# Linear attention and a Fourier feed-forward block on one core: the first part in a fixed written order, q loaded in 768-byte packets

## The chip, the core and the metric

One core of a Trainium2 chip runs the whole program. The metric is the device time of one execution in microseconds (us); lower is better. The core has five engines with a queue of instructions each (PE multiplies matrices, DVE, ACT and POOL work on vectors, SP only issues transfers), and 16 DMA engines move data.

## What is computed

```python
kv  = einsum('bhsd,bhse->bhde', k, v)        # q, k, v: 8 x 8 x 576 x 64, float32
out = einsum('bhsd,bhde->bhse', q, kv)
out = out / sqrt(mean(out*out, -1) + 1e-6) * g_norm
x   = out.transpose(0, 2, 1, 3).reshape(8, 576, 512)
u   = x + real(fft(fft(x, axis=1), axis=2))
un  = (u - mean(u)) / sqrt(var(u) + 1e-6)    # over the last axis
y   = u + maximum(un @ w_ch1, 0) @ w_ch2     # 512 x 2048 and 2048 x 512
```

## The kernel before

The program has two parts. The first goes through the 8 batches: for each it makes kv, turns q, multiplies the two, normalizes, does both Fourier transforms as matrix products, writes u, and turns u into the form the feed-forward block reads. Beside that it converts the first weight columns and does a first piece of the feed-forward block (three of 16 column groups) for all nine token blocks. The second part, from line L1791 on, does the rest of the feed-forward block. It is nearly all 512-column matrix products.

The first part is written as a list of operations (`op` and `dma` in class `Plan`), each with an engine, a rank and the operations it needs. `Plan.run` orders them: before, it walked a made-up time, kept a list of ready operations for each engine and took the one with the smallest rank; a table `SHIFT` moved the ranks. The order so found is fixed for each engine (`pin`), so that an engine takes its instructions strictly in that order. PE stands still where the next one in its order isn't ready, though a later one might be.

What PE does in the first part, by line:

- L798, `plan_spare`: "spare" 512-column products that nothing reads. 30 stand at the start (`WARM`), and further ones (`SPARE`, two lots of 40 and 22) have the lowest rank, so the plan puts them where nothing else is ready.
- L950, `plan_kv`: kv. An operation is one pair of heads, 12 products of 64 rows by 64 columns, which the profile records as 24. Each writes half of the columns of the array. ACT copies the result (`kvt`, L961); for batch 0 DVE also writes a copy times g_norm (L970).
- L1019, `plan_q`: q turned, four products by an identity, in plain float32. ACT copies the result into `fq` (L1023).
- L1046, `plan_out`: q times kv. 16 products (32 records), each of which reads 64 partitions, that is half of the rows of the array; the two heads of a pair lie in the two halves.
- L1280 (`plan_seq`), L1324 (`plan_chn`), L1422 (`plan_turn`), L685 (weights' mean): transforms, turning and the conversion of weights.
- L726 and L744 (`plan_early`): the 512-column products of the feed-forward block, in fp32r.

`plan_q_load` (L986, L994) loads q with `p j h d` on the tile's side: each packet is 64 floats, 256 bytes, one head of one token. In the loop over batches a `plan_q` is made for each j (token modulo 3), and `plan_out` for t needs the two q tiles of its own t.

Of the kernel before, what the change touches and what calls it, by code (L numbers as in the profile page):

```python
# [14 lines left out]
ALU = mybir.AluOpType  # L15
# [12 lines left out]
NA = 3  # L28
# [15 lines left out]
SPARE = ((40, 12000), (22, 38000))  # L44
# [10 lines left out]
SHIFT = {  # L55
    ("", "DVE", -100): -2880.5,
    ("", "POOL", -40): -937,
    ("", "SP DMA", -40): -23730.5,
    ("", "HOST", 0): -1181.5,
    ("", "POOL", 10): 24,  # L60
    ("", "SP DMA", 10): 294.5,
    ("", "POOL", 20): 552.5,
    ("", "SP DMA", 20): -63868.5,
    ("", "POOL", 30): 1213.5,
    ("", "POOL", 40): 1162.5,
    ("", "POOL", 50): 2073,
    ("", "POOL", 60): 3539,
    ("", "POOL", 70): 6370.5,
    ("", "DVE", 85): -240,
    ("", "PE", 85): 1946,  # L70
    ("", "SP DMA", 85): 991.5,
    ("", "HOST", 9000): 139.5,
    ("chn", "ACT", -34): 315,
    ("chn", "DVE", -34): 25,
    ("chn", "PE", -34): 3750.5,
    ("chn", "SP DMA", -34): 18885,
    ("chn", "ACT", 16): 1136,
    ("chn", "DVE", 16): 22530.5,
    ("chn", "PE", 16): 7,
    ("chn", "POOL", 16): -981.5,  # L80
    ("chn", "SP DMA", 16): -292,
    ("chn", "ACT", 26): 3465.5,
    ("chn", "DVE", 26): 18.5,
    ("chn", "PE", 26): -28.5,
    ("chn", "SP DMA", 26): -1643.5,
    ("chn", "DVE", 36): 36.5,
    ("chn", "PE", 36): -334.5,
    ("chn", "POOL", 36): -148,
    ("chn", "SP DMA", 36): -641.5,
    ("chn", "ACT", 46): 72966,  # L90
    ("chn", "DVE", 46): 404.5,
    ("chn", "PE", 46): -656,
    ("chn", "POOL", 46): 769,
    ("chn", "SP DMA", 46): 2653,
    ("chn", "ACT", 56): -555,
    ("chn", "DVE", 56): -1076,
    ("chn", "PE", 56): 57521.5,
    ("chn", "POOL", 56): -191.5,
    ("chn", "SP DMA", 56): -527,
    ("chn", "ACT", 66): -18.5,  # L100
    ("chn", "DVE", 66): 19,
    ("chn", "PE", 66): 259.5,
    ("chn", "POOL", 66): -733.5,
    ("chn", "SP DMA", 66): -1681.5,
    ("chn", "ACT", 76): 28.5,
    ("chn", "DVE", 76): 521,
    ("chn", "PE", 76): 1380.5,
    ("chn", "POOL", 76): -141,
    ("chn", "SP DMA", 76): 1068,
    ("dft", "POOL", -37): -79,  # L110
    ("dft", "SP DMA", -37): -552.5,
    ("dft_d", "ACT", -35): -1247.5,
    ("dft_d", "DVE", -35): 2333.5,
    ("dft_d", "POOL", -35): -601,
    ("dft_rest", "POOL", 9): 1006,
    ("dft_rest", "SP DMA", 9): 7159,
    ("dft_split", "ACT", -37): 22716,
    ("dft_split", "POOL", -37): 1615,
    ("dft_split", "ACT", 9): 73006,
    ("dft_split", "POOL", 9): -14.5,  # L120
    ("early", "ACT", -100): -25,
    ("early", "DVE", -100): 2547,
    ("early", "SP DMA", -100): 400,
    ("early", "PE", 1000): 43.5,
    ("early", "PE", 1010): 3621,
    ("early", "PE", 1030): 720,
    ("early", "PE", 1040): -417,
    ("early", "PE", 1050): 53.5,
    ("early", "PE", 1060): -22,
    ("early", "PE", 1080): 47.5,  # L130
    ("fold", "DVE", -36): -1056.5,
    ("fold", "DVE", 14): 381,
    ("fold", "DVE", 24): 647,
    ("fold", "DVE", 34): 185,
    ("fold", "DVE", 44): 345.5,
    ("fold", "DVE", 54): -1436,
    ("fold", "DVE", 64): 417.5,
    ("fold", "DVE", 74): 53.5,
    ("folds", "ACT", 14): 165.5,
    ("folds", "POOL", 14): 480.5,  # L140
    ("folds", "POOL", 24): 171,
    ("folds", "ACT", 34): -184.5,
    ("folds", "POOL", 34): -317.5,
    ("folds", "ACT", 44): 1688.5,
    ("folds", "POOL", 44): -766.5,
    ("folds", "ACT", 54): 1295,
    ("folds", "POOL", 54): -440.5,
    ("folds", "ACT", 64): -1095.5,
    ("folds", "ACT", 74): -52.5,
    ("folds", "POOL", 74): -932.5,  # L150
    ("kv", "ACT", -40): -43,
    ("kv", "ACT DMA", -40): 1273,
    ("kv", "PE", -40): 878,
    ("kv", "SP DMA", -40): -36291.5,
    ("kv", "ACT", 10): -555,
    ("kv", "PE", 10): -4098.5,
    ("kv", "SP DMA", 10): -7696,
    ("kv", "ACT", 20): -544,
    ("kv", "PE", 20): -203,
    ("kv", "SP DMA", 20): 2621.5,  # L160
    ("kv", "PE", 30): 578,
    ("kv", "SP DMA", 30): 17834,
    ("kv", "ACT", 40): 1666.5,
    ("kv", "PE", 40): 3652.5,
    ("kv", "SP DMA", 40): 29857.5,
    ("kv", "ACT", 50): -2667.5,
    ("kv", "PE", 50): -60,
    ("kv", "SP DMA", 50): 1468.5,
    ("kv", "ACT", 60): -718,
    ("kv", "PE", 60): 1184.5,  # L170
    ("kv", "SP DMA", 60): 74007,
    ("kv", "ACT", 70): 950.5,
    ("kv", "PE", 70): -1199.5,
    ("kv", "SP DMA", 70): 92268.5,
    ("out", "ACT", -58): 77092,
    ("out", "DVE", -58): 200,
    ("out", "ACT", -8): -22,
    ("out", "DVE", -8): -78,
    ("out", "ACT", 2): -7071,
    ("out", "DVE", 2): -1231,  # L180
    ("out", "ACT", 12): 1319.5,
    ("out", "DVE", 12): -606.5,
    ("out", "PE", 12): -981,
    ("out", "ACT", 22): 2327,
    ("out", "DVE", 22): 2275.5,
    ("out", "PE", 22): 277.5,
    ("out", "POOL", 22): 2917.5,
    ("out", "ACT", 32): -2157,
    ("out", "PE", 32): 418.5,
    ("out", "POOL", 32): 1264.5,  # L190
    ("out", "ACT", 42): -98,
    ("out", "DVE", 42): 374.5,
    ("out", "PE", 42): -402.5,
    ("out", "POOL", 42): 56580.5,
    ("out", "ACT", 52): -34,
    ("out", "DVE", 52): -197.5,
    ("out", "PE", 52): 4262.5,
    ("out", "POOL", 52): 2493,
    ("out", "PE", 62): 1265.5,
    ("out", "POOL", 62): -863.5,  # L200
    ("out", "PE", 72): -402.5,
    ("out", "POOL", 72): 2316.5,
    ("q", "ACT", -39): 70,
    ("q", "PE", -39): -2780,
    ("q", "POOL", -39): 1767,
    ("q", "PE", 11): 936.5,
    ("q", "POOL", 11): 250.5,
    ("q", "ACT", 21): -440,
    ("q", "PE", 21): -816,
    ("q", "POOL", 21): 2781,  # L210
    ("q", "ACT", 31): -127.5,
    ("q", "PE", 31): 3763.5,
    ("q", "POOL", 31): -635,
    ("q", "ACT", 41): 143.5,
    ("q", "PE", 41): -179,
    ("q", "POOL", 41): 154,
    ("q", "ACT", 51): 1602,
    ("q", "PE", 51): 620.5,
    ("q", "POOL", 51): 4526.5,
    ("q", "ACT", 61): 3768.5,  # L220
    ("q", "PE", 61): 1082.5,
    ("q", "POOL", 61): -550.5,
    ("q", "ACT", 71): 924,
    ("q", "PE", 71): 4825,
    ("q", "POOL", 71): 54,
    ("q_load", "SP DMA", -39): -23057.5,
    ("q_load", "SP DMA", -38): -28773.5,
    ("q_load", "SP DMA", 11): -1479.5,
    ("q_load", "SP DMA", 21): 1231,
    ("q_load", "SP DMA", 31): 8702,  # L230
    ("q_load", "SP DMA", 41): 19825,
    ("q_load", "SP DMA", 51): 22558,
    ("q_load", "SP DMA", 61): 68611,
    ("q_load", "SP DMA", 71): 72453.5,
# [124 lines left out]
class Plan:  # L359
# [81 lines left out]
    def run(self):  # L441
# [5 lines left out]
        need = {}  # L447
# [1933 lines left out]
```

## Time and profile before

| | |
|---|---|
| median of 3 runs | 961.81 us (960.96 to 961.81) |
| the profiled execution's own time | 962.68 us |
| its span, first to last instruction | 960.9 us |
| PE busy | 951.0 us, 99% of the span, 5934 matmuls |
| DVE, POOL, ACT busy | 683.9, 443.7, 383.6 us |
| chain that ended last | PE 94%, DMA 2%, DVE 2%, issue 1%, SPq 1% |

Busy time on PE holds whatever is in the array, useful or not, and a matmul's end is modelled, so 99% does not say that 99% is needed. The rate (how many matmuls in how many us) says more.

### The profile page before, as it was taken

What the parts mean: (1) busy time and instruction counts of PE and PEld (TensorE: products, weight loads), DVE (VectorE), ACT (ScalarE), POOL (GpSimd) and SP (SyncE); (2) the same over time, 40 slices, a digit from 0 to 9 for tenths busy, and PEclk for the clock granted to TensorE, in tenths of its full rate; (3) what the DMA queues carried; (4) which work ended last, traced back from release to release, by engine and by line L of the source; (5) the groups of instructions that cost most, each with busy time, mean ns of one, the idle gap of its engine ahead of it and who ended that gap; (6) DMA issues with size and microseconds to landing.
All of it is one profiled execution on the core that took longest, in us unless ns stands there. A gap on an engine that the chain in (4) does not pass through costs nothing.

```text
span 960.9 us, 15968 instructions
## 1 busy us (share of the span) xinstructions
PE 951.0 (99%) x5934; PEld 799.0 (83%) x5934; DVE 683.9 (71%) x1199; ACT 383.6 (40%) x719; POOL 443.7 (46%) x436
## 2 busy tenths in 40 slices
PE   9999999999999999999999999999999999999998
PEld 7888889888888888888888888888888888888886
DVE  4889776678797478999457967586757685675554
ACT  2666766758655233433314321351225212521110
POOL 3557778676764215556725044825472437210000
PEclk9999999999999999999999999999999999999999
DMA  9999995955447899988489397529643675213412
GB/s 241 224 225 270 234 296 156 307 125 197 152 151 247 323 335 339 339 302 299 169 341 330 116 376 252 206 66 310 238 154 105 232 279 194 89 66 135 184 63 88
DMA packets 112654, 210.39 MB, mean 219 GB/s; under 512 B 45292, under 2 KB 66688, under 8 KB 103616
## 3 DMA queue, kind: packets, MB, share of 16 engines
q1 hardware_dynamic: 109536, 199.92, 63.1%
q0 software_dynamic: 1920, 6.29, 1.8%
q10 hardware_dynamic: 1120, 3.15, 1.1%
q8 instruction: 47, 0.77, 0.3%
q14 instruction: 31, 0.25, 0.1%
HBM read 141.40 MB, written 67.93 MB: 218 GB/s over the span
## 4 chain that ended last, share of the span: by engine, by line
PE 94%; DMA 2%; DVE 2%; issue 1%; SPq 1%; POOL 0%; ACT 0%; DVEq 0%; POOLq 0%
PE acc L2188 23%; PE ps_h L2153 20%; PE ps_h L1791 11%; PE acc L1802 10%; PE acc L744 8%; PE ps_h L726 7%; PE ps_f L1280 3%; PE ps_o L1046 3%; PE ps_f L1324 2%; PE ps_k L950 2%; PE ps_s L798 2%; DMA vm<-in_v_dram 2%; PE ps_t L1422 1%; PE ps_q L1019 1%; DMA km<-in_k_dram 1%
## 5 line engine op out<-in xcount | busy, mean ns | idle before, releaser
L2188 PE MATMUL acc<-w2c,hh 128*128 128x512 f32 x640 | 197.7, 390 | 0.0
L739 DVE SCALAR_TENSOR_TENSOR hl<-ps_h,hh 128x512 fp32r<-128x512 f32 x144 | 98.5, 687 | 103.6 <-ACT hh L736 103.2
L736 ACT ACTIVATE hh<-ps_h 128x512 fp32r<-128x512 f32 x144 | 85.8, 597 | 216.4 <-PE ps_h L2153 89.9
L2188 PEld LDWEIGHTS acc<-w2c,hh 128*128 128x128 f32 x640 | 119.7, 188 | 25.4
L2198 DVE TENSOR_TENSOR us<-acc,us 128x512 f32<-128x512 f32 (+1 forms) x161 | 106.9, 681 | 42.3 <-PE acc L2188 41.9
L2188 PE MATMUL acc<-w2c,hl 128*128 128x512 f32 x320 | 124.5, 389 | 0.0
L2153 PE MATMUL ps_h<-t,w1c 128*128 128x512 f32 x480 | 115.3, 389 | 0.0
L2153 PEld LDWEIGHTS ps_h<-t,w1c 128*128 128x128 f32 x480 | 90.1, 188 | 18.7
L1824 POOL TENSOR_TENSOR us<-us,low 128x512 f32<-128x512 f32 x30 | 45.6, 1524 | 99.3 <-ACT low L1821 93.4
L2153 PE MATMUL ps_h<-b,w1c 128*128 128x512 f32 x360 | 91.2, 389 | 0.0
L2153 PEld LDWEIGHTS ps_h<-b,w1c 128*128 128x128 f32 x360 | 67.6, 188 | 14.0
L2188 PEld LDWEIGHTS acc<-w2c,hl 128*128 128x128 f32 x320 | 60.1, 188 | 12.4
L726 PE MATMUL ps_h<-unTh,w 128*128 128x512 f32 x216 | 67.6, 395 | 1.3 <-DVE hl L739 1.3
L744 PE MATMUL acc<-w,hh 128*128 128x512 f32 x216 | 67.8, 399 | 0.0
L1802 PE MATMUL acc<-w,hh 128*128 128x512 f32 x216 | 64.2, 390 | 0.0
L1791 PE MATMUL ps_h<-unTh,w 128*128 128x512 f32 x192 | 59.9, 393 | 0.0
L2019 POOL TENSOR_TENSOR z<-z,low 128x512 f32<-128x512 f32 x24 | 31.0, 1296 | 58.4 <-DMA low<-unT_scr 58.3
L1096 POOL TENSOR_TENSOR x<-x,gb 96x512 f32<-96x512 f32 (+1 forms) x36 | 46.1, 1302 | 10.6 <-ACT x L1063 10.4
L2170 DVE TENSOR_TENSOR ps_h<-ps_h,s 128x512 f32<-128x512 f32 x60 | 39.8, 693 | 13.8 <-PE ps_h L2153 13.2
L2255 ACT COPY s<-ps_h 128x512 f32<-128x512 f32 x20 | 11.7, 587 | 92.5 <-PE ps_h L2153 92.5
L726 PEld LDWEIGHTS ps_h<-unTh,w 128*128 128x128 f32 x216 | 39.7, 188 | 9.5 <-DVE hl L739 1.5
L1802 PEld LDWEIGHTS acc<-w,hh 128*128 128x128 f32 x216 | 40.5, 188 | 8.3
(207 smaller groups left out, 1969.1 us busy)
## 6 DMA issues: line engine op xcount, KB each, us to landing
w1c<-w_scr SPq DMA_DIRECT2D x13, 1792.0 KB
raw<-in_moe_w_ch_dram SPq DMA_DIRECT2D x32, 512.0 KB
w2c<-w_scr SPq DMA_DIRECT2D x14, 1024.0 KB
unT_scr<-unTh SPq DMA_DIRECT2D x9, 1024.0 KB
unT_scr<-unTl SPq DMA_DIRECT2D x9, 1024.0 KB
part_scr<-part SPq DMA_DIRECT2D x36, 256.0 KB
w_scr<-w1q SPq DMA_DIRECT2D x5, 1792.0 KB
km<-in_k_dram SPq DMA_DIRECT2D x29, 288.0 KB
```

The lines of the kernel that those rows point to most:

```text
L726: nc.tensor.matmul(ps, w[c][:, kc * P : (kc + 1) * P], unT[a][:, kc, :], start=(idx == 0), stop=(idx == 3 * KC - 1),)
L736: nc.scalar.activation(hh, ps, AF.Relu)
L739: nc.vector.scalar_tensor_tensor(hl, ps, 0.0, hh.bitcast(F32), ALU.max, ALU.subtract)
L744: nc.tensor.matmul(acc, hpair[a][:, i * P : (i + 1) * P], w[c], start=(first and n == 0), stop=(last and n == 2),)
L1096: nc.gpsimd.tensor_tensor(v_, v_, gb[:n].unsqueeze(1).to_broadcast([n, H, D]), ALU.mult)
L1791: nc.tensor.matmul(ps, w1_of(f, c, kc), unTs[j][a][:, kc, :], start=(idx == 0), stop=(idx == 3 * KC - 1),)
L1802: nc.tensor.matmul(acc, hpair[a][:, i * P : (i + 1) * P], w2_of(f, c), start=(first_ and n == 0), stop=(last_ and n == 2),)
L1824: nc.gpsimd.tensor_tensor(ut, ut, part, ALU.add)
L2153: nc.tensor.matmul(ps, w[:, A_OF[m], c, kc * P : (kc + 1) * P], b[:, a, kc * BT : (kc + 1) * BT], start=(fresh and idx == 0), stop=(done a ...
L2170: nc.vector.tensor_tensor(to, a, b, ALU.add)
L2188: nc.tensor.matmul(ps, hpair[a][:, i * P : (i + 1) * P], w2c[n][:, r, c], start=(idx == 0), stop=(idx == 5),)
L2198: nc.vector.tensor_tensor(ut[:, cols], ps[:, cols], ut[:, cols], ALU.add)
```

## The change

- `run` takes the operations in the order of a string `ORDER`, two digits an operation. `SHIFT` and the ready lists are gone. The made-up time stays, for the rings of buffers and for `pin`.
- `SPARE` has 33 and 10 in place of 40 and 22: 19 spares fewer. `WARM` stays.
- q lies in its tile as `p h j d`, so that a packet is three tokens of one head: 192 floats, 768 bytes. Batch 0 has two loads a side (by heads) in place of three (by token), the other batches one as before; the broadcast row loads three tokens.
- `plan_q` turns 128 of the 192 columns (j, d) of each pair, so that a tile `fq` holds two of six pieces (head, token); `plan_out` takes its piece from the half where it lies. For that kv must lie in both halves: `kvt` has two slots, and three copies a batch take the place of one (on ACT; for batch 0 also on DVE). There are still six q tiles a batch and 16 products an output.
- Rings: fq 6 for 4, kv 5 for 6, e2 4 for 5. `plan_chn` also waits for the row sums of x (`zs`).

```diff
-SPARE = ((40, 12000), (22, 38000))
+SPARE = ((33, 12000), (10, 38000))
...
+ORDER = (
+    "040G0Z1H4l1N0U0K0F0O0P0E0A05071b0I1M0R1G0M0W0D020X1j1i0T09060Q0B0C4m4x0V1K084n0S0L1O4o1P4p1I1J4q0N0J"
...
-        for o in self.ops:
-            if not o.after:
-                heapq.heappush(events, (0, o.n, "ready", o))
...
+        digits = [DIGITS.index(c) for c in ORDER]
+        order = [self.ops[64 * a + b] for a, b in zip(digits[::2], digits[1::2])]
...
+        for o in order:
+            t = max([0] + [a.done + (0 if a.eng == o.eng else self.HOP) for a in o.after]) + o.wait
+            t = max(t, free.get(o.eng, 0), port if o.port else 0)
...
+            self.pin(o.emit, t)
...
-        kvt = ring("kvt", qkv, [P, NPAIR, D], "kvt")
+        kvt = ring("kvt", qkv, [P, 2, NPAIR, D], "kvt")
...
+        parts = ((0, 0, 0, P), (1, 0, D, D), (1, D, 0, D))
...
+        done = [op("ACT", 370, rank(b, KV), keep(*part), mm, [ps, kvt]) for part in parts]
...
-        qt = ring("qt", qkv, [TR + 2, 3, DM], "qt")
+        qt = ring("qt", qkv, [TR + 2, H, 3, D], "qt")
...
+        src = q[b, :, t0 : t0 + HALF, :].rearrange("h (p j) d -> p h (j d)", j=3)
+        parts = 2 if b == 0 else 1
...
-                nc.tensor.transpose(view()[:, m, :], qt.t[:n, j, m * P : (m + 1) * P], ident[:n, :n])
+            flat = qt.t[:n].rearrange("p (c s) j d -> p c (s j d)", s=2)
...
+                        piece = 3 * s + (2 - t if side else t)
+                        on = slice(piece % 2 * D, (piece % 2 + 1) * D)
...
-                            fqs[side].t[half, m, :n],
-                            kvt.t[half, m],
+                            fqs[side][piece // 2].t[on, m, :n],
+                            kvt.t[on, (s + piece) % 2, m],
```

Three places show how the order moves. First PE's start. Before (`ps_s` a spare, `ps_k` kv, `ps_w` the weights' mean, `ps_q` q turned):

```order
L798 MATMUL ps_s<-still 128x512 x30
L950 MATMUL ps_k<-vm,km 64x64 x12
L685 MATMUL ps_w<-wa,mean_t 128x128 x4
L798 MATMUL ps_s<-still 128x512 x2
L950 MATMUL ps_k<-vm,km 64x64 x12
L798 MATMUL ps_s<-still 128x512
L950 MATMUL ps_k<-vm,km 64x64 x12
L798 MATMUL ps_s<-still 128x512
L950 MATMUL ps_k<-kvm 64x64 x12
L798 MATMUL ps_s<-still 128x512 x2
L1019 MATMUL ps_q<-ident,qt 128x96 x4
```

PE's start in the changed kernel:

```order
L485 MATMUL ps_s<-still 128x512 x26
L637 MATMUL ps_k<-vm,km 64x64 x24
L485 MATMUL ps_s<-still 128x512 x4
L372 MATMUL ps_w<-wa,mean_t 128x128 x4
L485 MATMUL ps_s<-still 128x512 x4
L711 MATMUL ps_q<-ident,qt 128x96 x12
L485 MATMUL ps_s<-still 128x512 x3
L637 MATMUL ps_k<-vm,km 64x64 x12
L637 MATMUL ps_k<-kvm 64x64 x12
```

The four pairs of batch 0 stood alone between spares; now they stand two and two, and the first q turns stand between them. Second, PE around the end of batch 1's kv (its last pair is the second `kvm` row). Before:

```order
L950 MATMUL ps_k<-kvm 64x64 x12
L798 MATMUL ps_s<-still 128x512 x10
L1019 MATMUL ps_q<-ident,qt 128x98 x4
L1019 MATMUL ps_q<-ident,qt 128x96 x8
L798 MATMUL ps_s<-still 128x512 x9
L1019 MATMUL ps_q<-ident,qt 128x96 x4
L798 MATMUL ps_s<-still 128x512
L1046 MATMUL ps_o<-kvt,fq 96x64 x16
```

The same place in the changed kernel:

```order
L485 MATMUL ps_s<-still 128x512
L637 MATMUL ps_k<-kvm 64x64 x12
L637 MATMUL ps_k<-vm,km 64x64 x12
L741 MATMUL ps_o<-kvt,fq 96x64 x16
L485 MATMUL ps_s<-still 128x512
L741 MATMUL ps_o<-kvt,fq 96x64 x16
L637 MATMUL ps_k<-vm,km 64x64 x12
L741 MATMUL ps_o<-kvt,fq 98x64 x16
L637 MATMUL ps_k<-vm,km 64x64 x12
```

Between batch 1's last pair and its first output stood 20 spares and four q turns; now one pair of batch 2 does. Third, the start of SP's queue of transfers. Before (`raw` weights, `km` and `kvm` k, `qt` q):

```order
L649 DMA raw<-in_moe_w_ch_dram 128x4x256
L649 DMA raw<-in_moe_w_ch_dram 128x1024
L790 DMA rowidx<-in_order_dram 128x36
L939 DMA km<-in_k_dram 96x2x384 x3
L939 DMA kvm<-in_k_dram 96x2x384
L986 DMA qt<-in_q_dram 96x8x64 x2
```

The start of SP's queue in the changed kernel:

```order
L336 DMA raw<-in_moe_w_ch_dram 128x4x256
L691 DMA qt<-in_q_dram 2x8x192
L626 DMA km<-in_k_dram 96x2x384 x2
L476 DMA gb<-in_g_norm_dram 128x64
L685 DMA qt<-in_q_dram 96x4x192 x2
L336 DMA raw<-in_moe_w_ch_dram 128x1024
L626 DMA kvm<-in_k_dram 96x2x384
L626 DMA km<-in_k_dram 96x2x384
```

One side of q now stands ahead of the second weights and of the last two pairs of k.

## Rows read from the trace of the kernel before

**Rows 1.** Windows: stretch; busy us (instructions) by engine; granted clock, DMA share, GB/s.

```profile
0.00:7.00 7.00, 5.05 (x12) 4.00 (x13) 0.54 (x5) 2.15 (x3) 1.11 (x9) 1.00 0.71 216
12.00:80.00 68.00, 65.43 (x941) 56.21 (x938) 56.26 (x114) 40.23 (x87) 34.93 (x52) 1.00 1.08 231
80.00:140.00 60.00, 59.26 (x665) 51.91 (x663) 46.60 (x96) 40.55 (x86) 45.44 (x52) 1.00 1.01 275
140.00:344.00 204.00, 202.99 (x1582) 176.15 (x1583) 147.17 (x310) 120.54 (x252) 122.95 (x135) 1.00 0.66 214
344.00:957.00 613.00, 613.00 (x2718) 506.87 (x2716) 429.46 (x671) 180.13 (x294) 237.59 (x190) 1.00 0.58 214
```

**Rows 2.** Waits of PE over the whole span: us in total, times, longest us.

```profile
PE ps_s L798 <- DVE still L793: 2.0, 1, 2.0
PE ps_h L726 <- DVE hl L739: 1.3, 1, 1.3
PE ps_k L950 <- issue: 1.1, 1, 1.1
PE ps_k L950 <- DMA vm<-in_v_dram: 0.6, 2, 0.4
PE ps_o L1046 <- DVE unTl L1434: 0.5, 2, 0.3
PE ps_k L950 <- DVE ss L1083: 0.4, 1, 0.4
PE ps_q L1019 <- DVE ss L1083: 0.4, 1, 0.4
```

**Rows 3.** Timeline of PE, pairs and q turns among spares: start us, us.

```profile
14.97 0.51 PE L798 MATMUL ps_s<-still 128*128 128x512 f32 x1
15.40 0.92 PE L950 MATMUL ps_k<-vm,km 96*64 96x64 f32 x24
16.25 0.50 PE L798 MATMUL ps_s<-still 128*128 128x512 f32 x1
...
18.10 0.49 PE L1019 MATMUL ps_q<-ident,qt 96*128 96x96 f32 x4
18.38 0.95 PE L798 MATMUL ps_s<-still 128*128 128x512 f32 x3
19.16 0.49 PE L1019 MATMUL ps_q<-ident,qt 96*128 96x96 f32 x4
```

**Rows 4.** Timeline of PE, three pairs together and two outputs together.

```profile
24.25 2.96 PE L1046 MATMUL ps_o<-kvt,fq 64*96 64x64 f32 x64
27.15 0.88 PE L1019 MATMUL ps_q<-ident,qt 96*128 96x96 f32 x8
...
160.85 2.32 PE L950 MATMUL ps_k<-vm,km 96*64 96x64 f32 x72
163.10 0.55 PE L1422 MATMUL ps_t<-ident,x 97*128 97x97 f32 x4
```

**Rows 5.** Timeline of PE, one output between 512-column products.

```profile
81.49 0.39 PE L726 MATMUL ps_h<-unTl,w 128*128 128x512 f32 x1
81.81 1.57 PE L1046 MATMUL ps_o<-kvt,fq 64*96 64x64 f32 x32
83.32 0.73 PE L726 MATMUL ps_h<-unTh,w 128*128 128x512 f32 x2
83.89 0.40 PE L726 MATMUL ps_h<-unTl,w 128*128 128x512 f32 x1
84.12 0.62 PE L726 MATMUL ps_h<-unTh,w 128*128 128x512 f32 x2
84.58 0.39 PE L726 MATMUL ps_h<-unTl,w 128*128 128x512 f32 x1
```

**Rows 6.** The tile kvt: duration ns min/median/max, first and last start us.

```profile
L961 ACT COPY kvt<-ps_k x8: 372/372/384, 17.6 to 200.6; 128x256 f32<-128x256 f32 x8
```

**Rows 7.** The page's line on DMA packets.

```profile
DMA packets 112654, 210.39 MB, mean 219 GB/s; under 512 B 45292, under 2 KB 66688, under 8 KB 103616
```

More of the change, by code (lines that the diff above doesn't have):

```diff
@@ L342 @@
+DIGITS = "0123456789ABCDEFGHIJKLMNOPQRSTUVWXYZabcdefghijklmnopqrstuvwxyz+-"
 GAIN_AT_ONCE = (1,)
 RINGS = {
-    "p8": 8, "part": 2, "unT": 2, "h": 2 * NA, "qt": 2, "fq": 4, "kvt": 2, "kv": 6, "kr": 2, "xst": 1, "x": 9, "raw": 2, "e2": 5, "wk": 2, "xhl": 3, "pt": 1, "two": 2, "far": 1,
+    "p8": 8, "part": 2, "unT": 2, "h": 2 * NA, "qt": 2, "fq": 6, "kvt": 2, "kv": 5, "kr": 2, "xst": 1, "x": 9, "raw": 2, "e2": 4, "wk": 2, "xhl": 3, "pt": 1, "two": 2, "far": 1,
 }
@@ new lines, in run @@
+        for o in order:
+            t = max([0] + [a.done + (0 if a.eng == o.eng else self.HOP) for a in o.after]) + o.wait
+            t = max(t, free.get(o.eng, 0), port if o.port else 0)
+            for b in o.bufs:
+                if b.t is None:
+                    first = min(slots[b.ring])
+                    slots[b.ring].remove(first)
+                    t = max(t, first)
+                    b.t = b.make() or True
+            self.pin(o.emit, t)
+            end = free[o.eng] = t + o.cost
+            if o.port:
+                port = end
+            if o.dma:
+                pipe = max(pipe, end + 1300) + o.lag
+                free[o.eng] = max(end, pipe - self.AHEAD)
+                end = pipe + 700
+            for b in o.bufs:
+                b.left -= 1
+                b.close = max(getattr(b, "close", 0), end)
+                if not b.left:
+                    slots[b.ring].append(b.close)
+            o.done = end
@@ L975, in plan_kv, with src, keep @@
-        scaled = op("DVE", 330, rank(b, KV), gain, mm + [i_gb], [ps, kvg])
-        return kvt, kvg, [done, scaled], ld
+        def src(lo, hi):
+            return ps.t[lo:hi, : NPAIR * D].rearrange("p (c t) -> p c t", c=NPAIR)
+        parts = ((0, 0, 0, P), (1, 0, D, D), (1, D, 0, D))
+        def keep(slot, to, lo, n):
+            return lambda: nc.scalar.copy(kvt.t[to : to + n, slot], src(lo, lo + n))
+        done = [op("ACT", 370, rank(b, KV), keep(*part), mm, [ps, kvt]) for part in parts]
@@ L978, in plan_q_load, with gain @@
+        if b:
+            return kvt, kvt, done, ld
+        kvg = ring("kvt", qkv, [P, 2, NPAIR, D], "kvt")
+        def gain(slot, to, lo, n):
+            return lambda: nc.vector.tensor_tensor(
+                kvg.t[to : to + n, slot], src(lo, lo + n),
+                gb[lo : lo + n].unsqueeze(1).to_broadcast([n, NPAIR, D]), ALU.mult,
+            )
+        done += [op("DVE", 330, rank(b, KV), gain(*part), mm + [i_gb], [ps, kvg]) for part in parts]
+        return kvt, kvg, done, ld
     def plan_q_load(b, side):
-        qt = ring("qt", qkv, [TR + 2, 3, DM], "qt")
+        qt = ring("qt", qkv, [TR + 2, H, 3, D], "qt")
@@ new lines, in plan_q_load @@
+        parts = 2 if b == 0 else 1
+        ld = []
+        for n in range(parts):
+            hs = slice(n * H // parts, (n + 1) * H // parts)
+            ld.append(dma(
+                597 / parts, rank(b, QT) + n / 4,
+                lambda hs=hs: nc.sync.dma_start(of(qt.t[:TR, hs]), src[:, hs]),
+                bufs=[qt],
+            ))
+        if not side:
+            ld.append(dma(
+                2, rank(b, QT),
+                lambda: nc.sync.dma_start(
+                    of(qt.t[TR:]), q[b, :, :3, :].rearrange("h j d -> h (j d)").partition_broadcast(2),
@@ L1005, in plan_q_load, with plan_q @@
         return qt, ld
-    def plan_q(b, side, j, qt, ld):
-        n = rows[0] if side == 0 and j == 0 else TR
+    def plan_q(b, side, m, qt, ld):
+        n = TR if side else TR + 2
         fq = ring("fq", qkv, [P, NPAIR, TR + 2], "fq")
@@ L1017, in turn @@
         def turn():
-            for m in range(NPAIR):
-                nc.tensor.transpose(view()[:, m, :], qt.t[:n, j, m * P : (m + 1) * P], ident[:n, :n])
+            flat = qt.t[:n].rearrange("p (c s) j d -> p c (s j d)", s=2)
+            for c in range(NPAIR):
+                nc.tensor.transpose(
+                    view()[:, c, :], flat[:, c, m * P : (m + 1) * P], ident[:n, :n]
+                )
         def take():
@@ L1026, in plan_q @@
         done.append(op("ACT", 490, rank(b, QT), take, [tr], [ps, fq]))
-        if side and j == 2:
+        if side and m:
             done.append(op(
@@ L1370, in plan_chn @@
         if b == 0:
-            adds = [op("DVE", 690, r, fn, pms, [x, pm], port=True) for fn in (add_l, add_r)]
+            adds = [op("DVE", 690, r, fn, pms + read, [x, pm], port=True) for fn in (add_l, add_r)]
         else:
-            adds = [op("POOL", 1240, r, fn, pms, [x, pm]) for fn in (add_l, add_r)]
+            adds = [op("POOL", 1240, r, fn, pms + read, [x, pm]) for fn in (add_l, add_r)]
         r0 = b * S + 1
@@ L1565 @@
         )
-        reds, gs, fqs = [], {}, {}
+        reds, gs, fqs, taken = [], {}, [], []
         for side in range(2):
             qt, loaded = plan_q_load(b, side)
-            for j in range(3):
-                fqs[side, 2 - j if side else j] = plan_q(b, side, j, qt, loaded[j])
+            made = [plan_q(b, side, m, qt, loaded) for m in range(3)]
+            fqs.append([f for f, _ in made])
+            taken.append([d for _, d in made])
         for t in range(3):
-            pair = [fqs[side, t] for side in range(2)]
-            d, gs[t] = plan_out(
-                b, t, [p[0] for p in pair], pair[0][1] + pair[1][1] + kvt_done + [one_row], kvt,
-                kvg, xs[t], ss,
-            )
+            need = sum((
+                taken[side][m] for side in range(2)
+                for m in sorted({(3 * s + (2 - t if side else t)) // 2 for s in range(2)})
+            ), [])
+            d, gs[t] = plan_out(b, t, fqs, need + kvt_done + [one_row], kvt, kvg, xs[t], ss)
             reds.append(d)
```

455 lines of the change are left out of this document (45 added, 410 removed).

## The prediction, made before the changed kernel ran

> **What bounds the kernel now.** I read the windows first, because PE is 99% busy on the page and busy time alone doesn't say what the array does. From 344 to 957 us PE is busy in all of 613 us with 2718 matmuls, nearly all of 512 columns [rows 1]: 613 / 2718 = 0.2255 us each, which is the rate of one such product. Nothing in the change touches this part, and it can only start earlier. So the question is the first 344 us. There PE is busy too (65.43 of 68 us at the least dense place after the start), but with three things that give no result: spares, stops at a change of the kind of product, and waits.
>
> The view of waits comes next. After the first one (2.0 us at the start, before any data, which stays) PE waits for 1.3 + 1.1 + 0.6 + 0.5 + 0.4 + 0.4 = 4.3 us in all [rows 2]. Two of these end at transfers or at "issue" on kv (0.6 and 1.1), the others at DVE. The DMA engines are full to 140 us (shares of 1.08 and 1.01; over 1 because packets overlap), then at two thirds [rows 1]. So up to about 80 us the data come too late for PE to be fed, and the plan fills PE with spares; from then on PE itself is the bound.
>
> Hence the sum: the time after is the time before, less the spares taken out, less the stops taken out, plus the difference in waits. Work that is merely moved in PE's order costs the same there.
>
> **The change part by part.**
>
> *Spares.* There are 92 before and 73 after, counted in the order: 19 fewer. One takes 0.226 us at the full rate. 19 x 0.226 = **4.3 us**, wholly on the path, as PE has no gap beside them.
>
> *Stops at a change of kind.* In rows 3 a spare and a pair of kv repeat every 16.25 - 14.97 = 1.28 us. Three pairs in one stretch take 163.10 - 160.85 = 2.25 us [rows 4]. One pair alone takes 16.25 - 15.40 = 0.85 us [rows 3], so a further pair costs (2.25 - 0.85) / 2 = 0.70 us, and 0.15 us belongs to the stretch, not to its pairs. The spare beside it takes 1.28 - 0.85 = 0.43 us in place of 0.226, another 0.20. A stretch that uses half the array thus costs 0.35 us over its work. The same for an output of q times kv: two together take 27.15 - 24.25 = 2.90 us [rows 4], one alone 83.32 - 81.81 = 1.51 us, so 0.12 us is the stretch's; the product ahead of it takes 81.81 - 81.49 = 0.32 us for 84.81 - 84.58 or 0.23, and the two behind it 0.57 for 84.58 - 84.12 = 0.46 [rows 5], which makes 0.12 + 0.09 + 0.11 = 0.32 us. I take 0.31, a little less, because some stretches stand beside q turns, where a spare's stop isn't paid twice. Counted over PE's order, half-array stretches fall from 44 to 24: 20 x 0.31 = 6.2 us. Against that, kv and outputs that now follow each other directly keep their own 0.13 us (8 such meetings for 5): +0.4 us. Plain float32 turns cost a little too: three spares between two of them take 19.16 - 18.38 = 0.78 us for 0.68, so a change there and back costs 0.10 us at most, and nothing at least, if the turns' own end overlaps what follows; I take 0.07. There are 50 changes into such a stretch and 57 out of one before, 69 and 70 after, so about 16 round trips more: +1.1 us. Sum: 6.2 - 0.4 - 1.1 = **4.7 us** less. Its bounds: 20 x 0.28 - 0.4 - 1.6 = 3.6 and 20 x 0.35 - 0.4 = 6.6.
>
> *q's packets.* The same bytes in a third of the packets: 36,864 of the 45,292 packets under 512 bytes [rows 7] are q's (8 batches x 2 sides x 96 x 3 x 8). No row prices one. Below, the gain for PE is nothing beyond the two terms above (earlier q is what lets spares go); above, it is all that ends at transfers or issue on kv, 0.6 + 1.1 = 1.7 us. I take nothing, since kv's transfers, not q's, end those waits, and keep 1.7 for the range. The Trainium skill ("DMA: Bandwidth & Descriptors", Specifications) says that transfers below 512 B miss line rate because of a read-modify-write. By it the 768-byte packets leave that class and the sum would be lower by the 1.7 us; this trace shows the packets and the full queues, but no price of one.
>
> *Three copies of kv.* ACT has 16 copies more, 0.37 us each [rows 6]: 6 us. ACT is busy 40.23 of 68 us and 40.55 of 60 us [rows 1], so they are hidden as work. As latency they are not always: after batch 1's last pair one pair (0.70 us) stands ahead of the first output, and three copies take 3 x 0.37 = 1.1 us. Wait there: 0.4 us, or up to 0.9 with a copy of q in ACT's queue between (the copies of q stand ahead of them in the order). Behind it queue all later products. Before, 20 spares and four turns covered it, so the copy cost nothing. Elsewhere the copies have some microseconds of products in front of the output. The two more on DVE for batch 0 have ten spares and more q turns between kv and the outputs.
>
> *Waits.* Between 0 (below) and what a denser order brings (above, see the rivals). I take as much as before, 4.3 us: the waits at the old places go with the old order, and new ones of the sort just priced appear. The smaller rings of kv and e2 can make a load or a fold start later; their price is part of this term. The row sums that the channel step now waits for stand before it in DVE's order; they cost nothing.
>
> **Sum.** 4.3 + 4.7 = 9.0 us less. The profiled execution took 962.68 us (span 960.9 and 1.8 around it), so 953.7 on its own; it lies 0.9 above the median of the runs, so the forecast for the median is 961.8 - 9.0 = **952.8 us**.
>
> **Rivals.**
>
> *The waits go as well.* If the earlier q and the hand-made order feed PE without a gap, 4.3 us more fall away: 948.5 us; with the upper bound of the stops' term (1.9 us more) 946.6, which I round to a floor of 947. For it: the loads are fewer packets, and from 140 us on PE idles 1.0 us in all [rows 1]. Against: the kvt wait above. Chance 0.22 (947 to 950.5).
>
> *DVE is late.* Counted in the order, 146 DVE instructions now stand ahead of the first remainder of a relu, 126 before: 20 more, at 56.26 / 114 = 0.49 us [rows 1] 9.9 us. DVE idles 12 us of the 68, so most fits if its inputs come early; if half does not, PE waits 5 us more: 957.8. Past 9.0 us it would undo the gain. For it: DVE ends four of the six waits after the start [rows 2]. Against: DVE's idle time lies just where q and kv come late. Chance 0.15 (955.5 to 960).
>
> *The clock falls.* From 2 to 7 us 12 products took 5.05 us busy, 0.42 us each [rows 1], the lower of the two levels (1.2 against 2.4 GHz); the granted clock in the row reads 1.00 there, so the spacing tells it. With 19 fewer products to fill with, a stall in the first 80 us could bring that rate back. Each 512-column product would cost 0.42 - 0.226 = 0.20 us more, and from 9.0 / 0.20 = 45 products on the change loses; a stretch of 80 gives 952.8 + 16 = 969. Against it: the longest stop before is 1.3 us [rows 2], in a place without spares, and the full rate went on. The Trainium skill ("TensorE: Matmul & The Clock Gate", Part 1) has the clock fall after idle time, which would be this rival; the trace shows the slow start, and no fall after it. Chance 0.06.
>
> **Chances.** The forecast's own case (950.5 to 955.5): 0.52. With the three rivals 0.95; the remaining 0.05 are waits of a kind not named, mostly on the long side. A difference of 0.2% (1.9 us) is about what a measurement of this kernel tells from none. Faster by more than that: 0.52 + 0.22 + 0.13 of the DVE case = 0.87. Same: 0.05. Slower: 0.08. The range runs from the floor of 947 to 959.5, which leaves out the upper end of the DVE case, the clock and the rest; the forecast's own range is 950.5 to 955.5.
>
> **What would show it.** The spares' group with 73 matmuls and a busy time lower by 4 to 5 us; kv and outputs in groups of 48 or more records with 0.70 and 1.39 us for each one added; PE's waits after the start between 3 and 6 us, one of about 0.5 us on an output ahead of batch 1; the second part's first product at about 335 us, for 344, and the rest of the same length, 613 us. The prediction is wrong if a wait of several us on DVE stands ahead of the first 512-column products at 80 us, if the products there take 0.42 us, or if the second part grows waits because its weights come no earlier than before.

## The result and the profile after

The changed kernel takes 975.16 us (median of 6 runs, 968.25 to 978.94), beside 961.97 for the kernel before on the same chip (960.96 to 963.08): 1.0129 times, 95% interval 1.009 to 1.0168. It is slower by 13 us, on the other side of the forecast. One of the six runs kept a mean granted clock of 0.998 and took 968.25 us, still 6.3 above before; the others have 0.985 to 0.993. Its profiled execution took 974.95 us, with a span of 973.1, 12.2 more than before.

The windows of the changed kernel: three of those of [rows 1], and below them a finer cut (busy us of PE, PEld, DVE, ACT, POOL; granted clock, DMA share, GB/s).

```profile
12.00:80.00 68.00, 63.47 (x792) 54.09 (x792) 47.16 (x96) 36.59 (x78) 33.41 (x56) 0.85 0.92 222
80.00:140.00 60.00, 55.63 (x668) 50.46 (x665) 45.62 (x90) 41.14 (x93) 41.32 (x48) 0.94 0.83 223
...
344.00:957.00 613.00, 613.00 (x2717) 506.56 (x2716) 428.33 (x677) 182.65 (x298) 238.31 (x190) 1.00 0.60 219
...
16.00:20.00 4.00, 2.20 (x47) 1.72 (x47) 0.68 (x1) 1.41 (x3) 2.41 (x5) 0.97 1.12 249
20.00:23.00 3.00, 3.00 (x19) 2.30 (x16) 2.00 (x4) 0.89 (x2) 0.00 (x0) 0.50 1.09 289
23.00:30.00 7.00, 5.63 (x83) 4.98 (x81) 3.98 (x8) 4.12 (x10) 2.00 (x2) 0.99 1.06 267
30.00:47.00 17.00, 17.00 (x147) 14.67 (x146) 9.06 (x17) 8.07 (x17) 7.30 (x17) 0.50 0.76 171
47.00:95.00 48.00, 44.49 (x698) 39.33 (x697) 43.43 (x87) 33.99 (x74) 33.30 (x44) 1.00 0.97 224
95.00:102.00 7.00, 5.95 (x37) 5.77 (x39) 5.79 (x12) 3.50 (x10) 2.45 (x4) 0.52 0.44 118
```

The granted clock, 1.00 throughout before [rows 1], falls to 0.50 (1.2 for 2.4 GHz) three times: at 20, 30 and 95 us. The second time it stays there for 17 us. The stretch that starts at 344 us is as dense as before (613 us busy, 2717 matmuls), and from the second part's first product to the end it is 616.9 us for 616.8. All the loss lies ahead of the second part: its first product (L1488) starts at 356.2 us, before (L1791) at 344.1.

The waits of PE, all over 0.2 us:

```profile
PE ps_t L1118 <- DMA km<-in_k_dram: 1.8, 1, 1.8
PE ps_k L637 <- DMA km<-in_k_dram: 1.8, 1, 1.8
PE ps_s L485 <- DVE still L480: 1.7, 1, 1.7
PE ps_q L711 <- DVE ss L779: 1.6, 1, 1.6
PE ps_o L741 <- ACT fq L717: 1.4, 1, 1.4
PE acc L431 <- DVE unTl L1130: 1.2, 2, 0.9
PE acc L431 <- ACT hh L423: 0.7, 1, 0.7
PE ps_o L741 <- ACT kvt L653: 0.5, 1, 0.5
PE ps_t L1118 <- POOL x L1059: 0.5, 1, 0.5
PE ps_o L741 <- DVE ss L779: 0.5, 1, 0.5
PE ps_q L711 <- DMA qt<-in_q_dram: 0.3, 1, 0.3
```

Leaving out the first one at the start, that is 10.3 us, for 4.3 before [rows 2]. In the timeline of PE the first two falls stand behind the waits on k and on `fq` (start us, us, instruction, the wait ahead and what ended it):

```profile
18.64 0.92 PE L637 MATMUL ps_k<-vm,km 96*64 96x64 f32 x24 [1.80 <-DMA km<-in_k_dram]
19.39 1.19 PE L637 MATMUL ps_k<-kvm 96*64 96x64 f32 x24
20.51 2.50 PE L485 MATMUL ps_s<-still 128*128 128x512 f32 x5
...
24.84 0.50 PE L711 MATMUL ps_q<-ident,qt 98*128 98x98 f32 x4
...
28.22 1.60 PE L741 MATMUL ps_o<-kvt,fq 64*98 64x64 f32 x32 [1.37 <-ACT fq L717]
...
30.30 2.83 PE L741 MATMUL ps_o<-kvt,fq 64*96 64x64 f32 x32
...
34.21 5.39 PE L741 MATMUL ps_o<-kvt,fq 64*96 64x64 f32 x64
```

Two outputs together take 5.39 us, for 2.96 before [rows 4].

By the timelines the first of these stops goes with the new order of transfers: SP issues the last pair of k for batch 0 at 10.81 us, behind two loads of q; before, its last one (`kvm`) went out at 8.18. The second isn't a late load: q is there and turned at 24.84 us, but two steps of the weights' conversion, the first of which waited for DVE, stand ahead of the copy into `fq` in ACT's order. SP's queue before, then in the changed kernel, and ACT there:

```profile
8.18 0.31 SPq L939 DMA_DIRECT2D kvm<-in_k_dram  x1
```

```profile
6.17 0.83 SPq L685 DMA_DIRECT2D qt<-in_q_dram  x2
...
10.81 0.31 SPq L626 DMA_DIRECT2D km<-in_k_dram  x1
```

```profile
26.65 0.60 ACT L1172 ACTIVATE w<-ps_a 128x512 fp32r<-128x512 f32 x1 [1.14 <-DVE ps_a L1168]
27.14 0.65 ACT L339 ACTIVATE wp<-raw 128x512 f32<-128x512 f32 x1
27.69 0.48 ACT L717 COPY fq<-ps_q 128x392 f32<-128x392 f32 x1
```

Where the 12.2 us are, by the rows: the 19 spares are 4.3 us less. The waits are 6.0 more (10.3 for 4.3). In the three low stretches PE is busy for 3.00 + 17.00 + 5.95 = 25.95 us; two outputs took 2.96 us at the full level for 5.39 there, so the same work would have taken some 14.3 us, and the low level costs about 11.7 (an estimate; a count by stretches that isn't shown here gave 11.9, the figure in the expectations below). That makes 13.4 us more for 12.2 measured. Stops at changes of kind, together with all gaps too short for the view of waits, are thus only some 1.2 us less, where the forecast had 4.7.

kvt and the packets answer to [rows 6] and [rows 7]:

```profile
L653 ACT COPY kvt<-ps_k x24: 353/369/374, 22.6 to 214.8; 64x256 f32<-64x256 f32 x16, 128x256 f32<-128x256 f32 x8
```

```profile
DMA packets 88045, 210.44 MB, mean 216 GB/s; under 512 B 8268, under 2 KB 42080, under 8 KB 79008
```

### The profile page after: what moved, and what is told of

The parts are those of the page before. It is cut to its first block, busy times and chain, and to the rows that moved or that the text cites. A ratio compares the mean times of both kernels' runs of the same rounds, so it can differ in the third digit from the quotient of the medians.

```text
span 973.1 us, 15881 instructions
## 1 busy us (share of the span) xinstructions
PE 956.9 (98%) x5915; PEld 804.6 (83%) x5915; DVE 677.8 (70%) x1201; ACT 387.0 (40%) x735; POOL 444.5 (46%) x444
## 4 chain that ended last, share of the span: by engine, by line
PE 88%; DVE 5%; ACT 2%; DMA 2%; POOL 1%; issue 1%; ACTq 0%; SPq 0%; DVEq 0%; POOLq 0%
PE acc L1885 22%; PE ps_h L1850 20%; PE ps_h L1488 10%; PE acc L1499 10%; PE acc L431 7%; PE ps_h L413 7%; PE ps_o L741 3%; PE ps_f L976 2%; PE ps_f L1020 2%; PE ps_t L1118 2%; PE ps_k L637 1%; PE ps_q L711 1%; DMA raw<-in_moe_w_ch_dram 1%; DMA vm<-in_v_dram 1%; DVE x L847 1%
## 5 line engine op out<-in xcount | busy, mean ns | idle before, releaser
L1488 PE MATMUL ps_h<-unTh,w 128*128 128x512 f32 x192 | 60.0, 393 | 0.0
L1952 ACT COPY s<-ps_h 128x512 f32<-128x512 f32 x20 | 11.7, 587 | 92.8 <-PE ps_h L1850 92.8
L741 PEld LDWEIGHTS ps_o<-kvt,fq 64*96 64x96 f32 (+1 forms) x864 | 43.3, 179 | 6.0 <-ACT fq L717 1.5
L741 PE MATMUL ps_o<-kvt,fq 64*96 64x64 f32 (+1 forms) x864 | 45.5, 265 | 2.4 <-ACT fq L717 1.4
```

The source lines that it names most:

```text
L741: nc.tensor.matmul(pss[s].t[:n, at : at + D], fqs[side][piece // 2].t[on, m, :n], kvt.t[on, (s + piece) % 2, m], start=True, stop=True,)
L1488: nc.tensor.matmul(ps, w1_of(f, c, kc), unTs[j][a][:, kc, :], start=(idx == 0), stop=(idx == 3 * KC - 1),)
```

## The experiments

Theory 1 at first: half-array outputs, standing together with too few spares between, bring the clock down. Rival: PE's waits do. The two were taken up first, with the packets and the spares by themselves.

**Spares between the outputs, and the same spares ahead of them.** `EXTRA` names a stage, the number of an operation in it, and how many spares go behind it; the rest of the order is untouched.

```diff
+EXTRA = (("out", 1, 3), ("out", 2, 2), ("out", 4, 3), ("out", 5, 3))   # between
+EXTRA = (("q", 5, 11),)                                                # ahead
```

> The changed kernel with 11 more 512-column spares (11 x 0.226 = 2.5 us of work), set between batch 0's outputs: four behind each output or pair of outputs, for one or two. Theory 1 (the granted clock falls at 30 us because the half-array outputs of batch 0 stand nearly alone there, and it stays low until 47 us): the granted clock is 1.00 from 30 to 47 us, the 8.5 us or so that the slow products cost there go, and the kernel takes about 975 - 8.5 + 2.5 = 969 us or less. Rival (the clock falls because of the stop of 1.4 us at 28 us ahead of them): nothing here fills that stop, the clock falls as before, and the time is 975 to 978 us.

> The changed kernel with the same 11 more spares, all ahead of batch 0's first output; the outputs stand together as in the changed kernel. They take the place of the 1.4 us stop, so about 1.1 us of them are new. Theory 1 (the row of half-array outputs): the clock falls all the same a few us into the outputs, and the time is about that of the changed kernel, 975 to 977 us. Rival (the stop): the clock holds through 30 to 47 us, and the time is about 975 - 8.5 + 1.1 = 968 us or less.

Measured: 976.22 us between (1.0151, interval 1.0135 to 1.0166), 978.07 ahead (1.0162, 1.0148 to 1.0176). Windows, first of the version with spares between, then of the one with spares ahead:

```profile
26.00:50.00 24.00, 22.53 (x184) 19.01 (x182) 9.15 (x18) 9.56 (x20) 9.29 (x18) 0.51 0.64 154
```

```profile
30.00:48.00 18.00, 17.93 (x303) 15.46 (x301) 14.51 (x28) 12.18 (x27) 10.97 (x25) 1.00 1.00 228
48.00:51.00 3.00, 0.21 (x8) 0.07 (x4) 3.00 (x7) 1.55 (x5) 0.43 (x1) 1.00 0.54 124
51.00:68.00 17.00, 16.86 (x179) 15.04 (x180) 10.53 (x22) 6.44 (x13) 8.60 (x11) 0.50 0.69 174
```

Theory 1 fell. With spares between, the level is low from 26 to 50 us all the same; with the stop filled and the outputs left together, it holds through all of them. But then PE comes to batch 1's kv at 48 us, DVE isn't there (a wait of 2.9 us), and the level falls behind that wait, for 17 us again. Filling one stop moved the loss to the next, and the 968 us or less that were expected of a filled stop did not come.

**q in 256-byte packets again.** Three loads by token in place of one, into the changed layout:

```diff
-lambda hs=hs: nc.sync.dma_start(of(qt.t[:TR, hs]), src[:, hs]),
+lambda hs=hs: [
+    nc.sync.dma_start(qt.t[:TR, hs, j],
+                      src[:, hs].rearrange("p h (j d) -> p j h d", j=3)[:, j])
+    for j in range(3)
+],
```

> The changed kernel with q loaded in packets of 256 bytes again (three transfers by token in place of one); the tile's layout, the order and the spares are the changed kernel's. By theory (the packets are worth next to nothing for PE; the time went to the clock and to waits): within 2 us of the changed kernel. Rival (768-byte packets are what feeds PE early): more waits on q and k before 80 us, and slower than the changed kernel by 3 us or more.

Measured: 976.93 us, 1.0169 (1.0148 to 1.0189), beside 1.0129 (1.009 to 1.0168) of the changed kernel: the medians are 1.8 us apart, the ratios 0.4% (3.8 us), and the intervals overlap. The falls stand at the same places. The old packets are not faster, so the new ones don't explain the loss; whether they gain a little isn't shown. The six smaller loads of q put the last pair of k off to 13.38 us, and the wait on k is 2.07 us for 1.80.

**The kernel before without its 19 spares at 38.7 to 44.2 us.** The operations stay in the order and issue nothing:

```diff
+            count[0] += 1
+            if not 50 < count[0] <= 69:
                 nc.tensor.matmul(ps.t, still, wide, start=True, stop=True)
```

> The kernel before without the 19 spares that it has at 38.7 to 44.2 us; the order of all else is left. The prediction's term for the spares alone: 19 x 0.226 = 4.3 us less, about 957.6 us, with the granted clock at 1.00. Rival (the spares hold the clock): the granted clock falls behind that place, and the time is at or above that of before; or the q and k that they waited for are late and 3 to 4 us of waits take their place, about 961 us.

Measured: 966.92 us, 1.0044 (1.003 to 1.0058): slower than with the spares. The timeline, and the windows around it:

```profile
38.68 1.22 PE L1023 MATMUL ps_q<-ident,qt 98*128 98x98 f32 x12
41.63 0.87 PE L1023 MATMUL ps_q<-ident,qt 96*128 96x96 f32 x4 [1.73 <-DMA qt<-in_q_dram]
...
42.91 2.83 PE L1050 MATMUL ps_o<-kvt,fq 64*96 64x64 f32 x32
...
47.14 5.49 PE L1050 MATMUL ps_o<-kvt,fq 64*96 64x64 f32 x64
```

```profile
30.00:41.00 11.00, 8.69 (x171) 7.65 (x169) 9.84 (x24) 6.34 (x16) 7.40 (x15) 1.00 1.11 220
41.00:61.00 20.00, 19.37 (x162) 17.69 (x163) 13.10 (x23) 10.19 (x22) 10.35 (x14) 0.50 1.01 206
```

The spares of the old order stood in a gap: without them PE waits 1.73 us for q; the level falls in this wait and stays low for 20 us. A stop and a fall like those of the changed kernel thus come in the kernel before from the missing spares alone, with no new layout and no new order. They cost 4.9 us here; the stops of the changed kernel are others, and this run doesn't price them.

**All 19 back at the first two stops; one long row of spares; POOL's products later; all of it.** The four share one chip. The third moves four operations of POOL's order behind two small ones (numbers are those of the operations):

```diff
+EXTRA = (("q", 2, 9), ("q", 5, 10))                    # nineteen back
+EXTRA = (("out", 2, 12),)                              # one row
+MOVE = (((547, 538, 556, 537), 560),)                  # POOL later
+EXTRA = (("q", 2, 9), ("q", 5, 10), ("kv", 7, 16))     # filled, with MOVE
```

> The changed kernel with the 19 spares back that it took out, at its own first two stops: 9 at the stop of 1.8 us at 16.4 us, 10 at the stop of 1.4 us at 26.6 us. Theory (a stop of PE, wherever the data or another engine are late, is what brings the granted clock down; spares are free where they only fill a stop): no low level before 45 us, and the two falls at 20 and 30 us go (9.9 us of the 11.9 that the low level costs), if no new stop takes their place; about 967 us. But PE then comes to batch 1's kv some us earlier, where it would wait for DVE for 3 to 5 us at 45 to 48 us, as it did with 11 spares at the second place only; then the clock falls behind that stop for some 15 us, and the time is 973 to 978 us. Rival (half-array products bring it down by themselves): the clock falls during batch 0's outputs all the same, at about 30 us, with no stop ahead.

> The changed kernel with 12 spares in one row behind batch 0's third output, at 33 us, where the granted clock is already low. Theory (what keeps it low is that half-array products and gaps make up most of the stretch; an unbroken row of 512-column products brings it back): the clock is back at 1.00 within the row or a few us behind it, at 37 to 40 us in place of 47; the row costs 12 x 0.3 = 3.6 us, the outputs behind it gain 5 to 6, so 972 to 974 us. Rival (once down, it stays for a time that does not depend on the work): back at 47 us as before, and the row costs 12 x 0.42 = 5 us: 979 to 980 us.

> The changed kernel with four products on POOL (x times g_norm of batch 1, 1.3 us each, in a row at 89.4 to 94.8 us) moved behind the next two small steps of POOL's order, so that they no longer run beside two sums on DVE (x plus pm, 510 columns) that took 5.0 us there for 0.69 each elsewhere. Theory (DVE is held up by POOL, and the two stops of PE of 1.8 and 1.6 us at 92 to 96 us, with the low clock of 6.8 us behind them, come from it): the two sums take 0.7 to 1.0 us each, the two stops go or shrink below 1 us, no low level at 95 us: 975 - 3.4 - 3.4 = 968 us, or up to 971 if the products on POOL are late for the next step of batch 1. Rival (the stops are those of transfers of k, as the view of waits names one): nothing changes at 92 to 96 us.

> The changed kernel with 35 more spares (9 and 10 at its first two stops, 16 ahead of the stop at batch 1's kv at 45 to 48 us) and the four products on POOL moved. Theory: no stop over 1 us and the granted clock at 1.00 to 140 us, though more spares run than before the change; the spares only take the place of stops: 975 - 11.9 (low level) - 3.4 (stops at 92 to 96 us) + 0 to 3 = 960 to 963 us. Rival (the spares cost what they take, 35 x 0.226 = 7.9 us, and the clock is not the matter): above 970 us.

Measured, beside 960.91 of before: 971.48 us (1.0099, 1.0082 to 1.0116), 973.79 (1.0131, 1.0098 to 1.0165), 972.42 (1.0115, 1.0098 to 1.0133), 968.95 (1.0089, 1.0061 to 1.0117).

With 19 back the time lies between the two that were expected (967, or 973 to 978). There is no low level until 54 us; it falls there behind a new wait on DVE of 1.1 us at batch 1's output, for 7 us, and once more at 92 us as in the changed kernel. The rival, half-array products by themselves, is excluded a second time.

The one long row was inconclusive: the same wait stood ahead of it (1.22 us on fq, at 28.8 us), but no fall followed in the profiled execution, so there was nothing for the row to end. The falls at 21 and 92 us came as in the changed kernel, and one at 58 us behind a wait of 1.0 us on DVE.

POOL's products were the cause at 92 to 96 us. The timeline of the changed kernel there, and then the same place with POOL's four products moved:

```profile
89.39 5.45 POOL L792 TENSOR_TENSOR x<-x,gb 96x512 f32<-96x512 f32 x4
90.37 5.02 DVE L1062 TENSOR_TENSOR x<-x,pm 96x510 f32<-96x510 f32 x2
91.60 0.33 PE L1118 MATMUL ps_t<-ident,x 96*128 96x96 f32 x2
93.77 0.38 PE L1118 MATMUL ps_t<-ident,x 96*128 96x96 f32 x2 [1.84 <-DMA km<-in_k_dram]
95.31 1.27 DVE L779 TENSOR_REDUCE ss<-ps_o 98x8 f32<-98x512 f32 x2
96.05 0.92 PE L711 MATMUL ps_q<-ident,qt 98*128 98x98 f32 x4 [1.56 <-DVE ss L779]
```

```profile
85.82 1.28 DVE L1069 TENSOR_TENSOR x<-x,pm 96x510 f32<-96x510 f32 x2
87.00 0.49 PE L1125 MATMUL ps_t<-ident,x 96*128 96x96 f32 x4
...
91.68 5.08 POOL L799 TENSOR_TENSOR x<-x,gb 96x512 f32<-96x512 f32 x4
```

Two sums on DVE take 5.02 us beside POOL's row and 1.28 without it. The view puts PE's wait of 1.84 us down to a transfer of k, but the product reads x, the first of which DVE has just finished, and in three other versions the view names DVE's x for the same wait (1.61, 1.93 and 1.20 us); with the products moved that wait is gone and no low level follows at 95 us. The Trainium skill ("SBUF — State Buffer", Who interferes with whom) says that a DVE instruction with two inputs in SBUF contends with a POOL instruction that reads SBUF; the trace agrees, 5.02 us for 1.28. The profiled execution took 968.1 us; the median of 972.4 is above the 968 to 971 expected, and its interval overlaps that of the changed kernel (1.009 to 1.0168), so a gain in time isn't shown. In the profile the level falls at 54 us now, behind a wait of 1.2 us on DVE at a place where the changed kernel had 0.5.

All stops filled and POOL moved, the granted clock is 1.00 from 12 to 140 us, and the kernel is still 8 us above before. The 960 to 963 expected were wrong: the clock was held, but the 35 spares (35 x 0.226 = 7.9 us) replaced waits only in part, and PE still waits 6.9 us behind the start, 5.0 of them for DVE and ACT. This run also answers for the stops at changes of kind, without the clock. Beside the kernel before it has 16 spares (3.6 us) and 2.6 us of waits more, 6.2 in all. Its median is 8.0 us above before, its traced span (966.3 for 960.9) 5.4: what is left is between 1.8 more and 0.8 less, not 4.7 less.

**How many spares a stop is worth, and what ends a low level.** From the kernel before again, without 11 or 15 of the 19 spares (8 or 4 are left directly ahead of the q turn that waited), and without all 19 but with 12 in one row behind the first output after the stop; and the changed kernel with the same number of spares as before and POOL moved:

```diff
-            if not 50 < count[0] <= 69:
+            if not 50 < count[0] <= 61:      # eleven fewer
+            if not 50 < count[0] <= 65:      # fifteen fewer
...
+EXTRA = (("q", 2, 8), ("q", 5, 6), ("kv", 7, 5))       # changed kernel, with MOVE
```

> The kernel before without 11 of the 19 spares at 38.7 to 44.2 us; the 8 that are left stand directly ahead of the q turn that waited 1.7 us for its transfer when all 19 were gone. Theory (a spare that fills a stop is worth its time, one more is pure cost; a stop is what brings the clock down): no stop over 0.5 us there, granted clock 1.00, and 11 x 0.226 = 2.5 us less than before, about 958.5 to 959.5 us. Rival (fewer spares lower the clock whether or not there is a stop): a low level behind 40 us and 963 to 967 us.

> The kernel before without 15 of the 19 spares; 4 are left ahead of the q turn. By theory a stop of 0.6 to 1.0 us remains there, too short to bring the clock down: 11 x 0.226 = 2.5 us less than before as with 11 fewer, since the other 0.9 us become a wait: about 959 us. Rival: this stop is enough already, the clock falls as with 19 fewer, and the time is about 966 us.

> The kernel before without the 19 spares (the granted clock fell at 41 us there and came back at 61.5), with 12 spares in one row behind the first output after that stop. Theory (half-array outputs and q turns keep the low level, an unbroken row of 512-column products ends it): the clock falls at about 41 us and is back by 52 us; the time is 963 to 966 us, for 966.9 without the row. Rival (the low level lasts as long as it lasts): back at 60 us or later, and 968 to 970 us.

> The changed kernel with 19 spares back (8, 6 and 5 at the three places of the version with 35), so 92 as before the change, and the four products on POOL moved. Theory (the stops, not the number of spares, are what counts; the changed order has some 7 us more of small waits on DVE and ACT behind 90 us): the granted clock at 1.00 or one short fall, and 35 - 19 = 16 spares less than the version with 35, of which at most half were on the path: 965 to 969 us, still above before. Rival (the fill was what cost the time): 960 us or less.

Measured, beside 961.72 of before: 959.95 us (0.9986, 0.9973 to 0.9998), 962.06 (1.0014, 0.9996 to 1.0032), 964.56 (1.0027, 1.0014 to 1.004), 972.11 (1.0081, 1.0047 to 1.0115).

Eleven fewer is the only version that is faster than the kernel before, by 1.8 us in the medians; its interval barely leaves out no gain. The eight left fill the stop (a wait of 0.2 us stays), and the others were cost alone. It was not all of the 2.5 us. In the profiled execution, at 963.17 us, the clock still falls further on, at 50 us, behind a wait of 1.35 us at a later output that the view puts down to nobody ("issue"); four of the twelve runs have a mean granted clock of 0.996 to 0.998. One more has 0.948 at 964.36 us, which fits no price of a fall found here and stays unexplained.

Fifteen fewer leaves a wait of 1.16 us, and 962.06 us lies between the 959 and 966 expected. In the profiled execution no fall followed. Of its ten runs, the two shortest, with a mean clock of 1.0, took 960.1 us, the three with 0.991 to 0.993 took 966.1 to 967.3. The same program falls in one execution and not in another; how long the waits were in those without a trace isn't known.

The row behind the stop worked. Its timeline, and the windows:

```profile
42.27 2.83 PE L1057 MATMUL ps_o<-kvt,fq 64*96 64x64 f32 x32
45.03 5.04 PE L808 MATMUL ps_s<-still 128*128 128x512 f32 x12
49.90 0.82 PE L1028 MATMUL ps_q<-ident,qt 96*128 96x96 f32 x8
```

```profile
39.00:50.00 11.00, 9.69 (x57) 7.80 (x56) 5.84 (x13) 4.03 (x9) 7.68 (x9) 0.53 0.99 186
50.00:62.00 12.00, 11.23 (x147) 10.35 (x146) 8.45 (x16) 8.29 (x19) 3.24 (x7) 1.00 0.92 192
```

The level is back by 50 us, where without the row it was low until 61; its ten runs have mean clocks of 0.995 to 1.0, the five without the row 0.989 to 0.991. With twelve spares more it is 2.8 us above before, for 4.9 without the row, each on its own chip; the two intervals overlap, so the gain in time is likely but not shown.

The last version was expected at 965 to 969 us, and its median is above. It fell in the profiled execution (0.53 from 29 to 47 us, behind a wait of 1.4 us on fq), and its six runs are the clearest price of a fall: two with a mean clock of 0.999 and 1.0 took 964.3 us, four with 0.989 to 0.991 took 972.0 to 974.1. One low stretch of the length traced, 17 us, costs 8 to 10 us. And with the clock held, and as many spares as before, the change is in these two runs still 2.6 us slower than before (964.3 for 961.7).

## Why the prediction was wrong

*Spares.* 73 are in the trace, and their 4.3 us are gone from PE's work.

*Stops at a change of kind.* The 4.7 us less were not found: about 1.2 by the rows of the changed kernel, and between 0.8 less and 1.8 more in the version whose clock held. The price came from places in the order before and was carried over to new meetings of kinds. Whether a stop costs less there, or new gaps too short for the view took it back, stays open.

*"Waits. I take as much as before."* This is the step that failed, and the fall of the clock (below) follows from it. They are 10.3 us by the view for 4.3. The argument was that waits at the old places go with the old order; it left out that the new order brings stops of its own and takes out what filled PE's time. The kernel before without its 19 spares shows the second: 1.73 us of wait for q, and 5 us slower. The changed kernel shows the first: k issued behind q (1.8 us), q's copy behind the weights' conversion on ACT (1.37), two sums on DVE beside POOL (1.84, and 1.56 behind it). Only the last was tested by moving the work. Load order and ACT's order as causes are read from the timelines; no run moved them back.

*"The clock falls", 0.06.* The right mechanism with far too small a chance, and nothing in the sum: it costs about 12 us. What spoke against it, that a wait of 1.3 us passed before without a fall [rows 2], is weak evidence: over these traces waits of 1.0 to 1.4 us were followed by a fall in some places (1.37 us on fq in the changed kernel, 1.1 us on DVE with 19 spares back) and not in others (1.3 us before, 1.22 us on fq with the one long row). Behind the start all of those of 1.7 us and more had a fall in them or close behind. The price was put at 0.2 us for each 512-column product; here it was mostly half-array outputs and q turns that ran at the lower level, for 17 us, which is why so short a wait costs so much. The 969 us of this rival held 16 us for the clock, against some 12 found, and nothing for the waits that bring it about. The sentence on the Trainium skill ("TensorE: Matmul & The Clock Gate", Part 1), that the clock falls after idle time, agrees with the traces in so far as all 22 falls in them came in a wait of PE of 1.0 us or more, or within 2.3 us of its end; that idle time decides it alone they don't show.

*"DVE is late", 0.15.* Also part of it, at other places. PE waits for DVE ahead of batch 1's kv or output where it gets there at full clock with no spares ahead (2.9 us, 1.1, 1.0 and 1.2 in four versions), and two sums were slowed by POOL. The 20 more instructions were not the reason found.

*q's packets.* Taken as nothing, with 1.7 us as the bound: the run with the old packets is 1.8 us longer by the medians, 3.8 by the ratios, and the intervals overlap. No error is shown here.

*Three copies of kv.* The one wait forecast is there: 0.5 us on kvt ahead of an output, and a median copy of 369 ns.

*The second part.* It takes 616.9 us for 616.8 to the end of the span, with no new waits of weights; right. Its start was forecast at 335 us and is 356.

What stays open: with the clock held the changed order is still 2.6 to 8 us slower than before, not 9 faster. It has more small waits on DVE and ACT behind 90 us (0.4 to 0.9 us each in the view). They were not taken apart; whether the smaller rings of kv and e2 cause some of them was not tried.

## What to carry to other kernels

Before taking out filler work, ask what it stands in front of: without it, is PE working or waiting? A filler in a gap cost nothing here, and the gap without it may cost the clock. Beside the kernel before on the same chip it was 4.9 us more with the wait of 1.7 us and 1.8 less with eight spares of the same length in it, 6.6 us in all or nearly four times the gap. Fill each gap just to its length, and where a gap can't be filled, let a row of dense products follow it rather than half-array ones.

When one engine's stop is filled, look at what it reaches earlier: here a filled stop uncovered the next one, on DVE.

## What the runs showed of the hardware

A low stretch lasted 3 us where five 512-column spares and two q turns followed (20 to 23 us), 17 to 24 us where half-array outputs with one to four spares between followed, and 10 us where twelve spares in a row came after one output. Four spares behind each output did not bring the level back. I had expected spares to do so in any arrangement.

One DVE sum of 96 x 510 with both inputs in SBUF took up to 3.34 us beside POOL's products, for 0.69 alone. In the changed kernel:

```profile
L1062 DVE TENSOR_TENSOR x<-x,pm x3: 691/1754/3341, 79.6 to 93.6; 96x510 f32<-96x510 f32 x2, 98x510 f32<-98x510 f32 x1
```

In the kernel before one of these sums (L1366, at 70.81 us) took 1.71 us beside a POOL product, and no wait of PE over 0.3 us stands behind it.
